# Forty drains of GpSimd between the scatters of a two-mixture kernel

## The chip, the cores and the metric

The kernel runs on one core of a Trainium2 chip. The metric is the device time of one execution in microseconds (us). A run is stated as the median of several executions. The engines are called as the profile calls them: PE is the matrix engine TensorE, DVE is VectorE, ACT is ScalarE, POOL is GpSimd, SP is SyncE. A "q" behind the name (POOLq, SPq) is the engine's sequencer, which fetches instructions, evaluates branches, waits for semaphores and handles some instructions by itself.

## What is computed

The reference has three stages. The first is attention over 8 batches and 8 heads, with keys and values averaged over groups of 8 positions. Its result, 4608 tokens of width 512, goes through a mixture of 8 experts, and the result of that through a second mixture of 8 experts. In each mixture a token goes to the one expert with the largest gate value:

```python
e_idx = np.argmax(logits, axis=1)
for e in range(E):
    mask = e_idx == e
    h = np.maximum(x[mask] @ w1[e], 0.0)
    out[mask] = gate_w[mask, None] * (h @ w2[e])
```

The first mixture has a second, sigmoid gate beside `gate_w`, the second adds a bias by modality to its gate values. Which tokens an expert gets is known on the chip alone, so the kernel sorts the tokens by expert: rows are written by indirect DMAs to places that the chip has computed.

## The kernel before, in words

The attention loop goes over 36 tiles of 128 tokens. When a group of tiles has been routed, `scatter1` (L496) issues one indirect DMA per tile on POOL, which writes the rows into `xs1`, a DRAM buffer with a region for each expert: 36 in all.

Each mixture goes over blocks of 256 sorted rows. `one(s)` (L1000) writes out the work of block `s`; blocks below 18 always run, the others stand in nested conditionals (`rest`, L1092), as many as the counts ask for. PE multiplies in two layers, each with operands split in a high and a low part, three products in place of one. ACT and DVE evict and split. A block's second half of 128 rows stands in a conditional too (`half2`).

POOL has four kinds of work in the mixtures. `bias_of` (L1030) is seven small operations on a block of the first mixture; the last of them, the copy on L865, writes into the row buffer `y`, of which there are two, and so waits for the scatter that read it before. `low2` (L1063, the operations are on L839) makes the low parts of an expert's second-layer weights, 16 operations, in a block that is an expert's last. `scatter()` (defined on L904, the DMA on L907, called on L1065) sends the rows of the block before into `xs2`, the input of the second mixture: one indirect DMA for the first half and one, under a condition, for the second. `write_out` (the DMA on L1080) sends a half block of the second mixture to the output: the first half on L1046, the second under a condition. Where a conditional skips an indirect DMA, the other branch has an INC_SWDGE_SEM on POOLq, which counts the skipped DMA's semaphore up.

The order of the instructions on each engine is the order of the program text. Within `one(s)` that is, for POOL in the first mixture: `bias_of` of block s, then `low2` if the block is an expert's last, then `scatter()` with the rows of block s-1. In the second mixture: `write_out` of the first half, `write_out` of the second, then `low2`.

The program ends with instructions on L1196, after the last line of the kernel's work: on every engine a drain, on SP waits for all semaphores, and barriers between them.

Of the kernel before, what the change touches and what calls it, by code (L numbers as in the profile page):

```python
# [47 lines left out]
def kernel(ctx, tc, q, k, v, wg, wo, w1, w2, mod, wg2, bias2, v1, v2, out):  # L48
    nc = tc.nc
    PE, ACT, DVE, GP, SP = nc.tensor, nc.scalar, nc.vector, nc.gpsimd, nc.sync  # L50
# [64 lines left out]
    def reg(ap, engines, hi):  # L115
        return nc.values_load(ap, engines=engines, min_val=0, max_val=hi, skip_runtime_bounds_check_because=SURE)  # L116
# [90 lines left out]
    def behind(group, ins):  # L207

        for name in placed[group]:
            tc.add_manual_dep(ins.ins, name, DATA, reason="rows that scatters wrote")  # L210
# [555 lines left out]
    def first_layer(xh, xl, between=None):  # L766


        kept = []

        def results(kk, p):
            ACT.activation(HH[kk], p, AF.Relu)  # L772
            DVE.scalar_tensor_tensor(HL[kk], in0=p, scalar=0.0, in1=HH[kk].bitcast(F32), op0=ALU.max, op1=ALU.subtract)  # L773

        after, early, here, then = between or (NF, None, None, None)
        trio = [(W1H, d, xh) for d in range(ND)] + [(W1L, d, xh) for d in (0, 2, 3)] + [(W1H, d, xl) for d in range(ND)] + [(W1L, 1, xh)]
        for kk in range(NF // 2):
            p = pm.tile([P, 2 * BLK], F32, name=f"h{kk}").rearrange("p (c s) -> p c s", c=2)
            for c2 in range(2):
                f = 2 * kk + c2  # L780
                c = f * P
                for n, (W, d, x) in enumerate(trio):
                    PE.matmul(p[:, c2, :], lhsT=W[d][:, c:c + P], rhs=x[:, d, :], start=n == 0, stop=n == 3 * ND - 1)  # L783
                if f == 0 and early:
                    early()
                if f == after:
                    here()
                    for k2, p2 in kept:
                        results(k2, p2)
            if early and 2 * kk + 1 < after:  # L790
                kept.append((kk, p))
                continue
            results(kk, p)
            if kk == after // 2:
                then()
# [21 lines left out]
    def second_layer(hf, p, apart=False):  # L817

        trio = ((HH, W2H), (HH, W2L), (HL, W2H))
        if apart:  # L820
            steps = [(f, trio[i]) for i, fs in ((0, range(NF)), (1, range(NF // 2)), (2, range(NF)), (1, range(NF // 2, NF))) for f in fs]
        else:
            steps = [(f, m) for f in range(NF) for m in trio]
        for i, (f, (X, W)) in enumerate(steps):
            PE.matmul(p, lhsT=X[f // 2][:, f % 2, hf * P:(hf + 1) * P], rhs=W[f // 2][:, f % 2, :], start=i == 0, stop=i == 3 * NF - 1)  # L825

    def weigh(p, hf, S):
        ACT.activation(S["y"][:, hf, 0:DM], p, AF.Copy, scale=S["xg"][:, hf, DM:DM + 1])  # L828

    def split1():  # L830
        for cs in (slice(0, F // 2), slice(F // 2, F)):
            for j in (0, 2, 3, 1):
                split_chunk(R1[j][:, cs], W1H[j][:, cs], W1L[j][:, cs], DVE)
# [15 lines left out]
    def dots(p, S, hf):  # L849


        for e in range(1, E):
            DVE.tensor_tensor_reduce(out=M["junk"][:, e % 2], in0=p, in1=M["wg2b"][:, e, :], scale=1.0, scalar=0.0, op0=ALU.mult, op1=ALU.add, accum_out=S["lg"][:, hf, e:e + 1])  # L853
# [62 lines left out]
    def mixture(m, rows, a1, a2, base, first, after):  # L916
# [20 lines left out]
        def fetch(s):  # L937
            if s >= SMAX:
                return
            if m == 1 and s > 1:  # L940
                DVE.memset(xg_of(s)[:, 1, DM + 1:DM + 2], float(N))
            with run(s, [ET.SP]):
                load_block(s, reg(tabs[0][s:s + 1, ROW:ROW + 1], [ET.SP], E * REG - BLK), half2(s, [ET.SP]))

        def turn_in(s):

            t = turned(pm, ("t0", "t1"))
            xh, xl = x_of(s)
            if s < SMAX:
                with run(s, [ET.PE]) as here:  # L950
                    turn(t, xg_of(s))
            if m == 1 and s >= SMIN:
                with here.Else() if s < SMAX else ExitStack():
                    turn(t, M["xg20"])

            def rest():
                with run(s, [ET.Activation, ET.DVE]) if m == 2 and s < SMAX else ExitStack():
                    if m == 1 or s < SMAX:
                        high(t, xh)
                        low(t, xh, xl)  # L960

            return rest
# [37 lines left out]
        def one(s):  # L1000

            S, T = RS[s % 2], RS[(s - 1) % 2]
            S["xg"] = xg = xg_of(s)
            if SMIN <= s + 1 < SMAX:
                goes_on[s + 1] = reg(tabs[1][s + 1:s + 2, RUN:RUN + 1], ALL, 1)
            if s > 0:
                fetch(s + 3)
                if s > 1:
                    left = turn_in(s + 1)
                p = pm.tile([P, DM], F32, name="y", bufs=2)  # L1010
                with half2(s, C3) as full:
                    first_layer(*x_of(s))
                    second_layer(0, p)
                with full.Else():
                    first_layer_half(*x_of(s))
                    second_layer(0, p, True)
                if s == 1:
                    left = turn_in(2)
                if m == 1:
                    choose(T)  # L1020
                left()
            with when(s, SPLIT1, W3):
                split1()
            if s == 0:
                p = pm.tile([P, DM], F32, name="y", bufs=2)
                second_layer(0, p)
                if m == 1:
                    turn_in(1)()
            if m == 1:
                bias_of(S)  # L1030
            else:
                DVE.tensor_copy(S["ti"], xg[:, :, DM + 1])  # L1032
            weigh(p, 0, S)
            if m == 1:
                if s > 0:
                    scatter = place(T, half2(s - 1, [ET.Pool]))
                if s == SMIN - 2:
                    (fav["order"], fav["ei"], fav["eh"]), fs = favourite(base2, 2)
                    for f in fs:
                        f()  # L1040
                if s == 0:
                    w = M["wg2b"]
                    DVE.tensor_tensor(w[:, 1:E], w[:, 1:E], w[:, 0:1].to_broadcast([P, E - 1, DM]), op=ALU.subtract)
                dots(p, S, 0)
            if m == 2:
                write_out(S, 0)  # L1046
            p1 = pm.tile([P, DM], F32, name="y", bufs=2)
            with half2(s, [ET.PE, ET.Activation, ET.Pool]) if s > 0 else ExitStack():  # L1048
                second_layer(1, p1)
                weigh(p1, 1, S)  # L1050
                if m == 2:
                    write_out(S, 1)
            if s == 0:
                if m == 2:
                    turn_in(1)()
                ahead()
            if m == 1:
                with half2(s, [ET.DVE]) if s > 0 else ExitStack():
                    dots(p1, S, 1)
            with when(s, SPLIT2, [ET.Activation, ET.Pool]):  # L1060
                for j in range(NF // 2):
                    ACT.activation(W2H[j], R2[j], AF.Copy)  # L1062
                low2(range(NF // 2))  # L1063
            if m == 1 and s > 0:
                scatter()  # L1065
            if m == 1 and s == SMIN - 2:
                fav["e"] = reg(fav["ei"][0:1, 0:1], [ET.SP], E - 1)
                row = reg(fav["ei"][0:1, 1:2], [ET.SP], (E - 1) * REG)
                behind("xs2", SP.dma_start(M["xg20"], xs2[ds(row, BLK), :].rearrange("(h p) c -> p h c", p=P)))
                with when(s, LASTE, [ET.SP]):  # L1070
                    load_raw(v1, v2, fav["e"])
            if s + 1 < SMAX:
                with when(s + 1, PF, [ET.SP]):
                    load_raw(a1, a2, reg(tabs[1][s + 1:s + 2, NX:NX + 1], [ET.SP], E - 1))
                if m == 1 and s + 1 >= SMIN - 1:
                    with when(s + 1, PLAST, [ET.SP]):
                        load_raw(v1, v2, fav["e"])

        def write_out(S, hf):
            apart("out", GP.indirect_dma_start(out, IDX(ap=S["ti"][:, hf:hf + 1], axis=0), S["y"][:, hf, 0:DM], None, bounds_check=N - 1, oob_is_err=False))  # L1080
# [120 lines left out]
```

## Time and profile before

| what | us |
|---|---|
| median of 3 runs (1117.98 to 1119.69) | 1118.88 |
| profiled execution, its own time | 1117.44 |
| span of the profile, first to last instruction | 1115.7 |
| PE busy | 1066.5 |
| DVE busy | 594.6 |
| ACT busy | 393.8 |
| POOL busy | 334.7 |

The profile counts an engine as busy while it computes. Register, branch, semaphore and drain instructions are not counted as busy; they appear in the views by line, under the engine's name with a q. A view by line gives for each kind of instruction the count, the shortest, median and longest duration in ns, and the start of the first and of the last. The view in order of time gives start and duration in us and, in brackets, how long the engine had been idle and what released it. The granted clock of TensorE is 0.991 of full speed over the span.

### The profile page before, as it was taken

How to read it: one execution, taken by the hardware profiler on the slowest of the kernel's cores; microseconds unless marked ns; L12 is line 12 of the kernel's file. 1: busy time of each engine (PE TensorE's matmuls, PEld its weight loads, DVE VectorE, ACT ScalarE, POOL GpSimd, SP SyncE). 2: the span in 40 equal slices, each digit the busy share in tenths (PEclk: the TensorE clock that was granted, in tenths of full speed). 3: DMA queues.
4: the chain of work that ended last, by engine and by line, in shares of the span. 5: the costliest groups of instructions: out<-in, count | busy, mean ns of one | idle time of the engine just before them, and what ended most of it. 6: DMA issues, size and time to landing. Idle time of an engine off the chain costs nothing. (4 is left out here: it accounts for less than half of the span.)

```text
span 1115.7 us, 21941 instructions
## 1 busy us (share of the span) xinstructions
PE 1066.5 (96%) x7058; PEld 961.6 (86%) x7058; DVE 594.6 (53%) x1839; ACT 393.8 (35%) x924; POOL 334.7 (30%) x563
## 2 busy tenths in 40 slices
PE   7998989999999999999999989999999999999993
PEld 6998888998888888888888878889998898889982
DVE  6889777768887667679866673211112222111120
ACT  6887872216354215236221151211212512111120
POOL 7566484113757215108312130011000140101000
PEclk9999999999999999999999989999999999999997
DMA  9877455613746114125511005511011211111000
GB/s 345 276 283 250 174 201 189 218 49 123 258 155 225 58 49 161 64 78 163 185 54 41 21 24 177 205 58 58 31 40 39 60 40 39 43 55 40 21 20 22
DMA packets 52096, 128.17 MB, mean 115 GB/s; under 512 B 6957, under 2 KB 10029, under 8 KB 51760
## 3 DMA queue, kind: packets, MB, share of 16 engines
q1 hardware_dynamic: 42928, 97.28, 26.7%
q0 software_dynamic: 8960, 28.47, 6.5%
q8 instruction: 88, 1.44, 0.5%
q14 instruction: 120, 0.98, 0.3%
HBM read 92.51 MB, written 34.27 MB: 114 GB/s over the span
## 5 line engine op out<-in xcount | busy, mean ns | idle before, releaser
L773 DVE SCALAR_TENSOR_TENSOR hl<-h,hh 128x512 fp32r<-128x512 f32 x140 | 95.3, 690 | 368.4 <-ACT hh L772 365.3
L825 PE MATMUL y<-W2H,hh 128*128 128x512 f32 x608 | 235.3, 398 | 2.8 <-ACT W2H L974 2.5
L825 PE MATMUL y<-W2L,hh 128*128 128x512 f32 x608 | 234.6, 395 | 0.5 <-POOL W2L L839 0.5
L825 PE MATMUL y<-W2H,hl 128*128 128x512 f32 x608 | 233.3, 395 | 0.0
L772 ACT ACTIVATE hh<-h 128x512 fp32r<-128x512 f32 x140 | 83.3, 596 | 312.4 <-PE h L783 309.2
L853 DVE CUSTOM_DVE_ANT_0 junk<-y,wg2b 128x512 f32<-128x512 f32 x273 | 169.5, 685 | 8.3 <-ACTq L1060 5.2
L828 ACT ACTIVATE y<-y,xg 128x512 f32<-128x512 f32 x76 | 52.3, 688 | 300.4 <-PE y L825 236.4
L1080 POOL DMA_INDIRECT out_dram<-y,ti x37 | 36.0, 973 | 380.1 <-ACT y L828 258.9
L825 PEld LDWEIGHTS y<-W2H,hh 128*128 128x128 f32 x608 | 114.0, 188 | 28.5 <-ACT W2H L974 2.5
L825 PEld LDWEIGHTS y<-W2H,hl 128*128 128x128 f32 x608 | 114.4, 188 | 26.8
L825 PEld LDWEIGHTS y<-W2L,hh 128*128 128x128 f32 x608 | 114.6, 188 | 26.0 <-POOL W2L L839 1.3
L839 POOL TENSOR_TENSOR W2L<-R,W2H 128x256 fp32r<-128x256 f32 x140 | 99.5, 747 | 84.5 <-ACT W2H L1062 82.2
L783 PE MATMUL h<-xH,W1L 128*128 128x256 f32 x608 | 123.7, 285 | 0.2 <-DVE W1L L193 0.2
L783 PE MATMUL h<-xH,W1H 128*128 128x256 f32 x608 | 100.4, 288 | 4.6 <-issue 3.8
L783 PE MATMUL h<-x2H,W1L 128*128 128x256 f32 x512 | 103.2, 282 | 0.1
L907 POOL DMA_INDIRECT xs<-y,qdi x39 | 39.8, 1020 | 203.3 <-DVE lg L853 190.0
L783 PE MATMUL h<-xL,W1H 128*128 128x256 f32 x608 | 98.5, 285 | 0.0
L783 PEld LDWEIGHTS h<-xH,W1L 128*128 128x128 f32 x608 | 95.8, 193 | 0.4 <-DVE W1L L193 0.4
L783 PEld LDWEIGHTS h<-xH,W1H 128*128 128x128 f32 x608 | 84.7, 194 | 5.0 <-issue 3.8
L783 PEld LDWEIGHTS h<-xL,W1H 128*128 128x128 f32 x608 | 84.6, 194 | 0.0
L783 PE MATMUL h<-x2H,W1H 128*128 128x256 f32 x512 | 83.8, 285 | 0.4 <-ACT x2H L245 0.4
L783 PE MATMUL h<-x2L,W1H 128*128 128x256 f32 x512 | 82.1, 282 | 0.0
(241 smaller groups left out, 1597.1 us busy)
## 6 DMA issues: line engine op xcount, KB each, us to landing
R<-in_w_dram SPq DMA_DIRECT2D x56, 512.0 KB, 4.7
xg<-xs SPq DMA_DIRECT2D x72, 258.0 KB, 2.7
kv<-in_v_dram SPq DMA_DIRECT2D x16, 576.0 KB, 4.5
R<-in_v_dram SPq DMA_DIRECT2D x16, 512.0 KB, 6.3
kv<-in_k_dram SPq DMA_DIRECT2D x14, 576.0 KB, 8.8
qt<-in_q_dram SPq DMA_DIRECT2D x14, 576.0 KB, 10.1
xs<-dummy SPq DMA_DIRECT2D x18, 258.0 KB, 3.5
wraw<-in_w_dram SPq DMA_DIRECT2D x8, 512.0 KB, 4.3
```

The lines of the kernel that those rows point to most:

```text
L772: ACT.activation(HH[kk], p, AF.Relu)
L773: DVE.scalar_tensor_tensor(HL[kk], in0=p, scalar=0.0, in1=HH[kk].bitcast(F32), op0=ALU.max, op1=ALU.subtract)
L783: PE.matmul(p[:, c2, :], lhsT=W[d][:, c:c + P], rhs=x[:, d, :], start=n == 0, stop=n == 3 * ND - 1)
L825: PE.matmul(p, lhsT=X[f // 2][:, f % 2, hf * P:(hf + 1) * P], rhs=W[f // 2][:, f % 2, :], start=i == 0, stop=i == 3 * NF - 1)
L828: ACT.activation(S["y"][:, hf, 0:DM], p, AF.Copy, scale=S["xg"][:, hf, DM:DM + 1])
L839: GP.tensor_tensor(W2L[j][:, c, w], R2[j][:, c, w], W2H[j][:, c, w].bitcast(F32), op=ALU.subtract)
L853: DVE.tensor_tensor_reduce(out=M["junk"][:, e % 2], in0=p, in1=M["wg2b"][:, e, :], scale=1.0, scalar=0.0, op0=ALU.mult, op1=ALU.add, accum ...
L907: apart("xs2", GP.indirect_dma_start(xs2, IDX(ap=di[:, hf:hf + 1], axis=0), y[:, hf, :], None, bounds_check=E * REG - 1, oob_is_err=False))
L1080: apart("out", GP.indirect_dma_start(out, IDX(ap=S["ti"][:, hf:hf + 1], axis=0), S["y"][:, hf, 0:DM], None, bounds_check=N - 1, oob_is_err ...
```

## The change

`GP.drain()` is an instruction on POOL's queue. The change adds two calls in `one(s)`: one in the second mixture ahead of the first half's `write_out`, one in the first mixture ahead of `scatter()`, in all blocks but the first. Nothing else is changed. The `scatter()` that `place` makes in `end` gets none.

```diff
             if m == 2:
+                GP.drain()
                 write_out(S, 0)
...
             if m == 1 and s > 0:
+                GP.drain()
                 scatter()
```

## Rows read from the trace of the kernel before

**Rows 1.** Stages: length; busy us of PE, PEld, DVE, ACT, POOL; clock; DMA share; GB/s.
```profile
669.00:1098.20 429.20, 425.85 (x2708) 383.72 (x2708) 85.39 (x176) 94.47 (x161) 47.24 (x53) 1.00 0.19 61
1098.20:1115.70 17.50, 0.00 (x0) 0.00 (x0) 0.00 (x0) 0.11 (x1) 0.97 (x1) 0.63 0.05 17
```

**Rows 2.** Order of time, the last work: start, us, what, idle before.
```profile
1097.19 0.40 PE L825 MATMUL y<-W2H,hl 128*128 128x512 f32 x1
...
1098.59 0.97 POOL L1080 DMA_INDIRECT out_dram<-y,ti  x1 [4.60 <-ACTq L1060]
```

**Rows 3.** By line, POOL's sequencer from 1100 us on: ns min/median/max, first and last start.
```profile
L1094 POOLq INC_SWDGE_SEM  x1: 2408/2408/2408, 1103.1 to 1103.1; - x1
...
L1196 POOLq DRAIN  x3: 46/107/9223, 1105.7 to 1115.5; - x3
```

**Rows 4.** By line, SP's sequencer from 1105 to 1110 us.
```profile
L1196 SPq EVENT_SEMAPHORE  x12: 28/28/28, 1105.5 to 1106.2; - x12
```

**Rows 5.** By line, all indirect DMAs, who waited for L907's (us, times), the output's landing.
```profile
L497 POOL DMA_INDIRECT xs<-x,rdi x36: 967/993/1240, 48.6 to 178.6; - x36
...
L907 POOL DMA_INDIRECT xs<-y,qdi x39: 967/1061/1066, 216.3 to 669.0; - x39
...
  ACT y L828: 23.7, 4
...
L1080 POOL DMA_INDIRECT out_dram<-y,ti x37: 971/972/993, 680.2 to 1098.6; - x37
...
DMA to landing us min/median/max: 2.7/3.6/3.6
```

**Rows 6.** By line, three other INC_SWDGE_SEM, and the scatters issued before them.
```profile
L1187 POOLq INC_SWDGE_SEM  x1: 31/31/31, 0.2 to 0.2; - x1
...
L907 POOL DMA_INDIRECT xs<-y,qdi x8: 967/1021/1066, 216.3 to 300.2; - x8
...
L906 POOLq INC_SWDGE_SEM  x1: 1074/1074/1074, 307.5 to 307.5; - x1
...
L1080 POOL DMA_INDIRECT out_dram<-y,ti x19: 971/972/980, 680.2 to 887.7; - x19
...
L1048 POOLq INC_SWDGE_SEM  x1: 2039/2039/2039, 888.0 to 888.0; - x1
```

**Rows 7.** By line, POOL's drain ahead of the kernel's work.
```profile
L1187 POOLq DRAIN  x1: 169/169/169, 0.4 to 0.4; - x1
```

**Rows 8.** By line, the instructions whose counts give the number of blocks.
```profile
L859 POOL TENSOR_SCALAR qnm<-xg x22: 186/211/757, 185.7 to 635.1; 128x2 f32<-128x2 f32 x22
...
L1032 DVE CAST ti<-xg x19: 165/169/1379, 679.2 to 1088.9; 128x2 int32<-128x2 f32 x19
```

**Rows 9.** Order of time, POOL in the second mixture, two scatters of results.
```profile
904.48 0.99 POOL L1080 DMA_INDIRECT out_dram<-y,ti  x1 [2.31 <-ACT y L828]
...
1093.01 0.97 POOL L1080 DMA_INDIRECT out_dram<-y,ti  x1 [17.19 <-ACT y L828]
```

**Rows 10.** By line, POOL's sequencer at L907 up to 307.4 us, and 524 to 527.
```profile
L907 POOLq EVENT_SEMAPHORE  x9: 17/17/23906, 191.6 to 306.8; - x9
...
L907 POOLq MOVE  x2: 29/29/29, 525.3 to 526.0; - x2
```

**Rows 11.** Order of time, POOL around two experts' ends in the first mixture.
```profile
287.42 11.27 POOL L839 TENSOR_TENSOR W2L<-R,W2H 128x256 fp32r<-128x256 f32 x16 [1.11 <-ACT W2H L1062]
...
513.88 1.06 POOL L907 DMA_INDIRECT xs<-y,qdi  x1 [0.16 <-ACT W1H L192]
...
520.69 0.56 POOL L865 COPY y<-xg 128x8 f32<-128x8 f32 x1 [0.64 <-DMA xs<-y,qdi]
522.22 11.26 POOL L839 TENSOR_TENSOR W2L<-R,W2H 128x256 fp32r<-128x256 f32 x16 [0.97 <-SPq L1073]
```

**Rows 12.** Order of time, PE's use of the last part of those weights.
```profile
299.90 0.40 PE L825 MATMUL y<-W2L,hh 128*128 128x512 f32 x1
...
534.20 0.40 PE L825 MATMUL y<-W2L,hh 128*128 128x512 f32 x1
```

## The prediction, made before the changed kernel ran

> **What bounds the kernel now.** I read the stages first, then the last work in order of time, then the instructions by line in the stretch in which no engine works, and at last POOL's own order in the mixtures.
>
> In the second mixture PE computes for 425.85 of 429.20 us [rows 1]. What POOL does there costs nothing as long as PE does not wait for it. But the last 17.5 us of the span hold no matmul at all [rows 1]: PE's last one starts at 1097.19, the last scatter of results at 1098.59 [rows 2], it lands at most 3.6 us later [rows 5], so by 1102.2, and the span ends at 1115.7. Some 13 us at the end are neither computation nor transfer.
>
> The views by line show whose they are. POOL's sequencer has an INC_SWDGE_SEM at 1103.1 that lasts 2.41 us, and from 1105.7 on three drains, of which the first lasts 9.22 us, to 1114.9; the other two, 0.11 and 0.05 us, lie in what is left up to 1115.7 [rows 3]. SP, which waits for the kernel's semaphores one after the other, has got through all twelve by 1106.2, 28 ns each [rows 4]: every transfer has landed by then. So for 8.7 us the drain is the one thing that the program's end waits for, and it waits for no data.
>
> What do these two instructions cost by? The kernel issues 36 + 39 + 37 = 112 indirect DMAs on POOL [rows 5]. INC_SWDGE_SEM lasts 1.07 us with 36 + 8 = 44 of them issued before it, 2.04 us with 36 + 39 + 19 = 94 [rows 6], and 2.41 us with all 112 [rows 3]. From the first to the last that is 1.334 us over 68 DMAs, 19.6 ns each; the line gives 2.05 us at 94, where the row has 2.04. It goes by the number of DMAs issued. The drain before the kernel's work, with none issued, lasts 0.17 us [rows 7]; the one behind 112 lasts 9.22 us. If its price too goes by the count, it is 9.05 / 112 = 81 ns for each.
>
> **The change part by part.** The first mixture runs `bias_of` for 22 blocks and the second casts its indices for 19 [rows 8]. The first block of the first mixture has no scatter, so 21 + 19 = 40 drains are added. A block issues one or two indirect DMAs. I take a drain to strike the entries of finished DMAs from a list that grows with each DMA, so that later instructions find the list short. The row at the end is the only long drain here, so that is a reading and not yet shown.
>
> *The end.* The last added drain stands ahead of the last block's first scatter. Behind it come two DMAs. The final drain then lasts 0.17 + 2 x 0.081 = 0.33 us in place of 9.22. SP is late next: its waits end 0.7 to 0.8 us behind the INC_SWDGE_SEM (1105.5 to 1106.2 [rows 3, 4]), and the drain only 0.5 us behind it. From the drain's end to the end of the span it is 1115.7 - 1114.9 = 0.8 us, and stays.
>
> *The INC_SWDGE_SEM ahead of it.* If it goes over the same list, it falls to the line's value at two DMAs, 1.074 - 42 x 0.0196 = 0.25 us; the shortest row is 0.03 us [rows 6]. I take 0.2, so it ends at 1103.3 and no longer at 1105.5. If it counts all DMAs of the execution, it stays at 2.41.
>
> *Sum.* 1103.3 + 0.8 (SP) + 0.8 (end) = 1104.9 of span in place of 1115.7: 10.8 us less. With the INC_SWDGE_SEM unchanged it is 1105.5 + 0.8 + 0.8 = 1107.1, 8.6 less.
>
> *The drains in the second mixture.* Each costs POOL 0.17 + 2 x 0.081 = 0.3 us by the count, and holds its sequencer until the engine is idle and, at worst, until the DMAs before it have landed (3.6 us [rows 5]). The scatter behind it has POOL idle 17.19 us ahead of it in the last block, and 2.31 us where `low2` stands before it [rows 9], waiting for ACT's result. Both cover 0.3 us, and behind `low2` the earlier DMAs have long landed. Cost nothing; without the cover, nobody in the second mixture waits for a scatter of results but the end.
>
> *The drains in the first mixture.* The first one strikes the 36 entries of `scatter1`: 0.17 + 36 x 0.081 = 3.1 us. POOL's sequencer waits up to 23.9 us at the scatters for DVE [rows 10], which hides that and the later drains of 0.3 us. It is different where `low2` runs directly before the drain. There the sequencer now runs ahead: it prepared the two scatters at 525.3 and 526.0, while `low2` was still running until 533.48 [rows 10, 11]. With the drain it must wait for the last `low2` operation and 0.33 us more, and then prepare the scatter; today that gap is 0.16 us [rows 11]. I bound the shift from 0.3 us (the preparation hidden in today's gap) to 1.0 us (preparation of both scatters exposed, 0.7 us apart in rows 10), and take 0.4, by the drain's row. Behind the scatter on POOL are `bias_of`, whose copy at 520.69 waits for the landing, and where two experts end in a row the next `low2`, 522.22 [rows 11]. PE waits for that: its use of what the last two operations write starts at 534.20, and `low2` ends at 522.22 + 11.26 = 533.48: a slack of 0.72 us. At the other such place it is 299.90 - (287.42 + 11.27) = 1.21 us [rows 11, 12]. A shift of 0.4 is hidden at both; at 1.0 the first costs 0.3 us. ACT waits four times for a scatter's landing, 23.7 us in all [rows 5], and would wait 0.4 longer; PE has a second `y` buffer to go on with, so I count nothing. The INC_SWDGE_SEM within the mixtures (1.07 and 2.04 us in rows 6) get shorter too, which can give back no more than PE idles: 429.20 - 425.85 = 3.35 us in the whole second mixture [rows 1]. At those two PE goes on as before, so I count none. Together: 0, from -1.2, a third of that idle time, to +1.
>
> The Trainium skill states on the page "PSUM — Partial Sum Buffer", section "Engine vs sequencer instructions", that a drain waits for the engine to go fully idle. The trace does not bear that out as the whole of it: POOL's last work ended at 1099.56, 6.1 us before the 9.22 us drain began [rows 2, 3]. By that rule alone the final drain would be no shorter and the sum would be nothing.
>
> **The sum against the runs.** The profiled execution took 1117.44 us, 1.7 more than its span, and would take 1106.6. The median of the runs is 1118.88; less 10.8 that is 1108.1. I forecast 1108.1 us.
>
> **The rivals.**
>
> *The INC_SWDGE_SEM stays.* For it: it is a count of DMAs issued in every row, and no drain stands between any two of them to show what a drain does to it. Against: it is simplest if both walk one list. Time 1118.88 - 8.6 = 1110.3.
>
> *The end is fixed.* The 9.22 us could be a cost of ending the program that has nothing to do with the count; there is one such row, and INC_SWDGE_SEM's slope is another instruction's. Against: the two drains behind it are also of POOL and of the end, and take 0.11 and 0.05 us [rows 3]. Time 1118.9, no change. The Trainium skill, page "Runtime: NRT & Kernel Launch", section "The ~15µs preamble/postamble breakdown", describes barriers and resets around any kernel by stage, about 9 to 15 us in total; by that table the end would stay. It names no stage that grows with the kernel's DMAs.
>
> *Each drain walks all DMAs issued so far* (slower). Then nothing is struck off, the final drain stays 9.22 us, and the drains in the body grow. At 513.88 some 36 + 25 DMAs have been issued (25 of the 39 by their even spread over 216.3 to 669.0 [rows 5]): 0.17 + 61 x 0.081 = 5.1 us, against 0.72 us of slack: PE loses 4.4. Ahead of 287.42 it is 36 + 5, 3.5 us, less 1.21 is 2.3. Time 1118.9 + 6.7 = 1125.6. It decides from the point where the drain ahead of 513.88 is longer than about 0.7 us. For it: a walk over everything issued is what INC_SWDGE_SEM's rows look like. Against: a drain that left nothing cleared would have to be 9 us again right behind the first one at the end, where they take 0.11 and 0.05.
>
> *The body costs more than it seems.* A drain that takes 2 us and not 0.3 for a few DMAs would push both `low2` places: 1.3 + 0.8 = 2.1 us. Time 1110.2.
>
> **How the numbers follow.** Chances: the forecast 0.67, the INC_SWDGE_SEM stays 0.13, the body costs more 0.05, the end fixed 0.08, each drain walks all 0.07. A difference of about 0.2%, 2.2 us, is what a measurement of this kernel can tell from none. The first three are faster by more than that: 0.85. Same 0.08, slower 0.07. The range takes in the first three: below, the forecast less the 1.2 and the runs' own scatter (0.9 either way), 1106.0; above, 1110.3 with the body's +1 and the scatter, 1112.3. That leaves out 0.15 and a little at the edges.
>
> **What would show it.** In the changed kernel's rows by line: the last POOL drain well under 1 us and the last INC_SWDGE_SEM near 0.2; SP's last waits, and no longer POOL's drain, directly ahead of the end; some 6 us from the last scatter of results to the end of the span and not 17; the forty drains about 0.3 us each and the first of them about 3; the scatter behind `low2` some 0.5 us behind its end; PE's gaps in the mixtures as before. The prediction is wrong if the final drain is still several us long, if the drains in the body grow along the kernel, or if PE waits for `low2` behind 522.22.

## The result and the profile after

The changed kernel takes 1109.48 us (median of 4 runs, 1108.82 to 1110.16), the kernel before, run beside it, 1119.29 us. The ratio is 0.9908 with a 95% interval of 0.9888 to 0.9928: faster by some 10 us. The forecast was 1108.1 us, with a range of 1106.0 to 1112.3.

| what | before, us | after, us |
|---|---|---|
| profiled execution, its own time | 1117.44 | 1110.16 |
| span of its profile | 1115.7 | 1108.4 |
| last matmul ends | 1097.6 | 1101.3 |
| from there to the end of the span | 18.1 | 7.1 |
| PE busy | 1066.5 | 1068.8 |

The table already shows two things: the end has become 11.0 us shorter, and TensorE finishes 3.8 us later. The first is what was forecast. The second was not.

The stage at the end, the whole second mixture beside it; columns as in [rows 1]:

```profile
669.00:1101.40 432.40, 427.57 (x2712) 385.11 (x2710) 86.50 (x192) 95.27 (x162) 47.37 (x54) 1.00 0.18 61
1101.40:1108.40 7.00, 0.00 (x0) 0.00 (x0) 0.00 (x0) 0.67 (x1) 0.97 (x1) 0.64 0.12 42
```

By line, the count instruction (INC_SWDGE_SEM) behind the last blocks, POOL's drains at the end and SP's waits, from three answers on three lines (columns: ns min/median/max, first and last start); they answer to [rows 3, 4]:

```profile
L1096 POOLq INC_SWDGE_SEM  x2: 213/214/215, 671.9 to 1106.3; - x2
...
L1198 SPq EVENT_SEMAPHORE  x14: 17/28/393, 1106.4 to 1108.4; - x14
...
L1198 POOLq DRAIN  x3: 46/107/208, 1106.7 to 1108.2; - x3
L1198 SPq DRAIN  x3: 7/7/13, 1107.6 to 1107.9; - x3
```

The longest of the three drains of POOL at the end takes 0.21 us where it took 9.22, and the INC_SWDGE_SEM 0.215 where it took 2.41. POOL's drain is over at 1106.9. SP's waits go on to 1107.5 (one of them lasts 0.39 us) and its drain comes at 1107.6, so SP is now late, as the prediction said it would be.

The added drains, by line, the first mixture's and then the second's. An indirect DMA is called open here as long as no drain has come behind it, whether it has landed or not:

```profile
L1066 POOLq DRAIN  x21: 122/218/8468, 190.5 to 642.2; - x21
...
L1046 POOLq DRAIN  x19: 302/2164/7853, 678.2 to 1080.4; - x19
```

Of the 21 in the first mixture 13 take 0.12 to 0.22 us. The shortest, with one indirect DMA since the drain before, lasts 0.12 us, those with two 0.21, and the first, with 36, 3.02 us: about 0.05 us and 0.083 us for each DMA. Seven of them last 8.4 to 8.5 us. These stand behind `low2`: the sequencer reaches the drain while `low2` is running and stays there until its last operation is over. POOL in order of time around two such places, then the scatter's line and the drain's line:

```profile
509.45 4.95 POOL L839 TENSOR_TENSOR W2L<-R,W2H 128x256 fp32r<-128x256 f32 x7
515.52 1.06 POOL L907 DMA_INDIRECT xs<-y,qdi  x1 [1.12 <-DVE qkm L879]
...
523.09 0.19 POOL L865 COPY y<-xg 128x8 f32<-128x8 f32 x1 [1.75 <-DMA xs<-y,qdi]
524.62 11.25 POOL L839 TENSOR_TENSOR W2L<-R,W2H 128x256 fp32r<-128x256 f32 x16 [1.34 <-ACT W2H L1063]
537.00 1.06 POOL L907 DMA_INDIRECT xs<-y,qdi  x1 [1.12 <-DVE qkm L879]
```

```profile
L907 POOLq MOVE  x2: 29/29/29, 514.7 to 515.4; - x2
...
L1066 POOLq DRAIN  x1: 8435/8435/8435, 506.2 to 506.2; - x1
```

`low2` ends at 509.45 + 4.95 = 514.40, the drain at 506.2 + 8.44 = 514.6, and only then does the sequencer begin on the scatter (the first MOVE, 514.7). The scatter starts at 515.52, so POOL has idled 1.12 us where it idled 0.16 before [rows 11]. The releaser that the view names, DVE's `qkm`, is not the cause, although it is ready only at 515.39, shortly ahead of the scatter. In the kernel before the scatter does not wait for it: it starts at 513.88 [rows 11], and that `qkm` comes behind it:

```profile
514.54 0.17 DVE L879 TENSOR_REDUCE qkm<-qa 128x2 f32<-128x16 f32 x1
```

So the time is the sequencer's own. The next `low2` then starts at 524.62, 2.40 us later than before [rows 11]. Of that, 0.68 us was there ahead of the drain (the `low2` in front of it ends at 514.40 and ended at 513.72). TensorE now reaches the products of `low2` first:

```profile
534.53 0.50 PE L825 MATMUL y<-W2L,hh 128*128 128x512 f32 x1 [0.18 <-POOL W2L L839]
...
535.93 0.50 PE L825 MATMUL y<-W2L,hh 128*128 128x512 f32 x1 [0.43 <-POOL W2L L839]
...
537.34 0.18 PE L886 MATMUL h<-oh,tri_b 128*128 128x16 bf16 x1 [0.68 <-DVE oh L881]
...
537.88 0.50 PE L825 MATMUL y<-W2H,hh 128*128 128x512 f32 x1 [0.31 <-issue]
```

This is the order of time of PE with the idle time before each in brackets: 1.60 us in four waits. The last of them, 0.31 us, the kernel before has too (0.30). The third, for DVE's `oh`, belongs to `low2` as well. DVE in order of time in the same stretch:

```profile
531.27 4.77 DVE L874 SCALAR_TENSOR_TENSOR qlg<-lg,y,bs 128x8 f32<-128x8 f32 x2
...
537.11 0.17 DVE L881 TENSOR_TENSOR oh<-qa,va 128x16 bf16<-128x16 f32 x1
```

Two small operations take 4.77 us there and end at 536.04; the first of them takes 4.63 and ends at 535.90, with `low2` (524.62 + 11.25 = 535.87); the median one takes 0.22 us. The kernel before shows the same, and how little room it left:

```profile
530.59 2.92 DVE L874 SCALAR_TENSOR_TENSOR qlg<-lg,y,bs 128x8 f32<-128x8 f32 x1
...
534.72 0.18 DVE L881 TENSOR_TENSOR oh<-qa,va 128x16 bf16<-128x16 f32 x1
```

```profile
534.95 0.18 PE L886 MATMUL h<-oh,tri_b 128*128 128x16 bf16 x1
```

There the operation on L874 ends at 533.51, with `low2` (533.48 [rows 11]), `oh` is written by 534.90, and TensorE takes it at 534.95. So `low2`'s end reaches TensorE by two ways, by its own products and by `oh`, and the second had 0.05 us of slack. Not every operation of DVE is held up like this: the 26 on L773 that ran beside `low2` took 0.67 to 0.69 us, as the others do.

In the second mixture the first drain lasts 0.30 us, with three open DMAs, the one behind `low2` 7.9, with one, and the others 1.4 to 4.3 us, with two each. Take one of these. The second half's scatter starts at 1055.06 and lands 2.7 us after its issue, by 1057.8; the drain that follows runs from 1056.5 to 1057.9. It waits for the landing: here and in twelve others of the nineteen the drain ends 0.12 us behind it.

```profile
1055.06 0.97 POOL L1082 DMA_INDIRECT out_dram<-y,ti  x1 [4.60 <-ACTq L1061]
1073.03 0.97 POOL L1082 DMA_INDIRECT out_dram<-y,ti  x1 [17.00 <-ACT y L828]
```

The next scatter starts at 1073.03 and has 17.00 us of POOL's idle time ahead of it, for ACT. That is the cover the prediction named; it hides 2 us as it would 0.3.

### The profile page after: what moved, and what is told of

It is laid out like the page before. It is cut to its first block, busy times and chain, and to the rows that moved or that the text cites. A ratio compares the mean times of both kernels' runs of the same rounds, so it can differ in the third digit from the quotient of the medians.

```text
span 1108.4 us, 21981 instructions
## 1 busy us (share of the span) xinstructions
PE 1068.8 (96%) x7058; PEld 963.7 (87%) x7058; DVE 594.1 (54%) x1839; ACT 393.6 (36%) x924; POOL 333.4 (30%) x563
## 5 line engine op out<-in xcount | busy, mean ns | idle before, releaser
L773 DVE SCALAR_TENSOR_TENSOR hl<-h,hh 128x512 fp32r<-128x512 f32 x140 | 95.3, 690 | 366.3 <-ACT hh L772 365.0
L907 POOL DMA_INDIRECT xs<-y,qdi x39 | 39.8, 1021 | 209.7 <-DVE lg L853 194.4
```

The source lines that it names most:

```text
L907: apart("xs2", GP.indirect_dma_start(xs2, IDX(ap=di[:, hf:hf + 1], axis=0), y[:, hf, :], None, bounds_check=E * REG - 1, oob_is_err=False))
```

## The experiments

Two questions were open: what in the body takes back part of the gain, and by what the end's price goes. All ratios are to the kernel before on the same chip.

**The change again, beside its parts.** Theory A: where the drain stands behind `low2`, it holds the sequencer, the scatter and the next `low2` come late, and TensorE loses about 2 us. Theory B: the loss was a lower clock of that one execution.

> The changed kernel again, as the measure for the others of this call. 9.8 us under the kernel before (ratio 0.991). Theory A: two places where low2 follows the scatter of the block before cost it about 2 us of PE's time, because POOL's sequencer prepares the scatter only behind the drain; PE's waits for W2L and for oh show again. Theory B: that loss was this one execution's lower clock, and another execution does not show it.

Measured: 1109.78 us (6 runs), ratio 0.9927 (0.9912 to 0.9943); before 1117.98. TensorE's waits near 302 and from 536 to 539 us are there again.

**The drains of the second mixture alone.**

```diff
             if m == 1 and s > 0:
-                GP.drain()
                 scatter()
```

> Drains in the second mixture alone. Both theories: the first of them strikes 75 entries (0.05 + 75 x 0.083 = 6.3 us), the last drain and INC_SWDGE_SEM are as short as with the change (0.2 us each). Theory A: no wait of PE behind low2 is added in the first mixture, so it is 11 us under the kernel before and 1 to 2 us under the changed one. Theory B: the same time as the changed one, 9.8 under.

Measured: 1109.2 us, ratio 0.991 (0.9895 to 0.9924). The waits in the first mixture are gone. The time is not told apart from the whole change's.

**The drain of the first mixture ahead of `low2`.** The same number of drains, none behind `low2`.

```diff
+            if m == 1 and s > 0:
+                GP.drain()
             with when(s, SPLIT2, [ET.Activation, ET.Pool]):
...
             if m == 1 and s > 0:
-                GP.drain()
                 scatter()
```

> Both groups of drains, those of the first mixture ahead of the condition with low2 and not behind it. Theory A (the sequencer held behind low2 costs): the scatters start 0.2 us behind low2 again, PE's added waits go, 10.5 to 11 us under the kernel before. Theory B: the same as the changed one.

Measured: 1107.03 us, ratio 0.9906 (0.9891 to 0.9921). POOL in order of time at the place shown above:

```profile
508.45 5.66 POOL L839 TENSOR_TENSOR W2L<-R,W2H 128x256 fp32r<-128x256 f32 x8
514.27 1.06 POOL L907 DMA_INDIRECT xs<-y,qdi  x1 [0.16 <-ACT W1H L192]
...
522.90 11.27 POOL L839 TENSOR_TENSOR W2L<-R,W2H 128x256 fp32r<-128x256 f32 x16 [1.26 <-ACT W2H L1065]
```

The scatter is back at 0.16 us behind `low2`, the kernel before's gap. The busy time of PE by stretch, first the kernel with the whole change run again, then this one, then the one with a single drain (below), settles Theory A at this place:

```profile
290.00:310.00 20.00, 19.02 (x112) 16.19 (x111) 14.28 (x41) 6.68 (x12) 14.13 (x25) 1.00 0.71 235
525.00:545.00 20.00, 18.61 (x107) 15.30 (x106) 15.40 (x48) 5.88 (x11) 14.71 (x25) 1.00 0.16 50
```

```profile
290.00:310.00 20.00, 20.00 (x117) 17.21 (x116) 13.10 (x41) 4.20 (x8) 13.00 (x23) 1.00 0.66 209
525.00:545.00 20.00, 20.00 (x125) 17.62 (x124) 15.77 (x55) 4.24 (x9) 15.02 (x31) 1.00 0.18 55
```

```profile
525.00:545.00 20.00, 20.00 (x125) 17.55 (x124) 15.53 (x55) 4.25 (x8) 13.53 (x28) 1.00 0.20 64
```

From 525 to 545 us TensorE idles 1.39 us with the drain behind `low2` (1.60 in the first profile of the change) and not at all with it ahead; the granted clock is 1.00 in every row, so Theory B does not account for these waits. The seven other traces agree: 0.86 us with the first mixture's drains alone, at most 0.42 in those without a drain behind `low2`, the kernel before included. From 290 to 310 us the picture is less clean: 0.57 to 0.98 us with it, but 0 to 1.17 without, because in two of these (38 more and 2 more, below) about 1 us of waiting that the other traces have near 281 us is absent and a wait comes behind 298 us instead. The first mixture as a whole, 220 to 640 us, parts the two groups. First the whole change run again, then the kernel with the drain ahead of `low2`:

```profile
220.00:640.00 420.00, 412.91 (x2641) 365.90 (x2640) 312.22 (x1004) 144.85 (x264) 149.13 (x284) 1.00 0.34 113
```

```profile
220.00:640.00 420.00, 415.72 (x2645) 370.00 (x2644) 309.84 (x1007) 145.22 (x263) 149.51 (x280) 0.99 0.34 113
```

TensorE idles 6.6 to 7.1 us there in the three traces with a drain behind `low2` (the change twice, and the first mixture's drains alone), and 4.1 to 5.2 in the eight without, of which the kernel before has the 5.2: 6.8 against 4.4 in the mean, 2.4 us apart. Both places have a part in it: from 220 to 310 us it is 2.4 to 3.1 with it and 1.5 to 2.2 without.

In time, the six runs of the whole change have a mean of 1110.4 us and the five of this kernel 1107.7; the difference of 2.7 us has an interval of 0.7 to 4.7, worked out from their scatter. This is the weaker evidence: in its first measurement the changed kernel had a ratio of 0.9908, no worse than the 0.9906 of this one.

**One drain only**, in the second mixture two blocks ahead of the end.

```diff
             if m == 2:
-                GP.drain()
+                if s == SMIN - 1:
+                    GP.drain()
                 write_out(S, 0)
...
             if m == 1 and s > 0:
-                GP.drain()
                 scatter()
```

> One drain in the whole program, in the second mixture's block 17, ahead of its first scatter. If a drain strikes the finished entries off a list, it lasts about 9 us in POOL's idle time, four scatters follow, the last drain is 0.05 + 4 x 0.083 = 0.4 us and the whole is 10.8 to 11 us under the kernel before. If the end were fixed, or every scatter needed its drain, it would be no faster than the kernel before.

Measured: 1107.21 us, ratio 0.990 (0.9886 to 0.9914). By line, the drain, the count instructions and the end:

```profile
L1047 POOLq DRAIN  x1: 8897/8897/8897, 1052.8 to 1052.8; - x1
...
L1096 POOLq INC_SWDGE_SEM  x2: 248/950/1653, 669.9 to 1103.1; - x2
...
L1198 POOLq DRAIN  x3: 46/107/381, 1103.5 to 1104.7; - x3
```

The 8.90 us have moved to 1052.8, into POOL's wait of 17 us, and behind them four DMAs are left: 0.38 us. One drain gives the whole gain of the end. By the scatter of its runs it is 3.3 us under the whole change in the mean (interval 1.5 to 5.1); against the one with the drains ahead of `low2` nothing can be told.

**The drains of the first mixture alone.**

```diff
             if m == 2:
-                GP.drain()
                 write_out(S, 0)
```

> The drains of the first mixture alone, those of the second left out. If a drain costs 0.05 us and 0.083 us for each indirect DMA of GpSimd since the last drain, and the count instruction 0.21 us and 0.0196 us for each (fitted to the trace of the changed kernel), the last drain here has the 37 indirect DMAs since the last drain before it: 0.05 + 37 x 0.083 = 3.1 us, and the count instruction 0.21 + 37 x 0.0196 = 0.93 us. The tail behind TensorE's last matmul is then 18.1 - (9.2 - 3.1) - (2.4 - 0.9) = 10.5 us. Theory A (the drains behind the low2 products hold the sequencer and cost TensorE some 1.4 us at 535-538 us and 0.6 us at 301 us): TensorE's waits of 0.4 and 0.7 us behind low2 are there as in the changed kernel, the span is about 1115.7 - 7.6 + 2 = 1110 us, and the time about 5.6 us under the kernel before. Theory B (those waits were that execution's alone): they are absent and the time is 7.6 us under it. Rival for the end (it costs the same however many DMAs are open): last drain 9.2 us, no gain.

Measured: 1112.18 us, ratio 0.995 (0.9938 to 0.9963), 5.7 us under the kernel before, where 5.6 was expected.

```profile
L1095 POOLq INC_SWDGE_SEM  x2: 213/592/972, 670.2 to 1104.6; - x2
...
L1197 POOLq DRAIN  x3: 52/111/3412, 1106.2 to 1110.2; - x3
```

The expectation left out three DMAs: behind the last added drain come the two of its own `scatter()`, one that `place` makes in `end`, and the 37 of the second mixture, so 40 are open. The last drain takes 3.41 us (0.05 + 40 x 0.083 = 3.4) and the count instruction 0.97 (0.21 + 40 x 0.0196 = 0.99). The end's price goes by the number since the last drain, and the rival of a fixed end falls. That the time came out as expected is in part luck, since the end was forecast 0.3 us too short.

**38 more indirect DMAs and no drain.** This should have been the mirror image: two more ahead of each block's first `write_out`, with indices out of bounds, so that they write nothing.

```diff
+    away = cst.tile([P, 1], I32, name="away")
+    GP.iota(away, [[1, 1]], base=OOB, channel_multiplier=1)
...
             if m == 2:
+                for _ in range(2):
+                    apart("out", GP.indirect_dma_start(out, IDX(ap=away, axis=0), dummy[:, 0:DM], None, bounds_check=N - 1, oob_is_err=False))
                 write_out(S, 0)
```

> The kernel before, without any drain, with two more indirect DMAs of GpSimd ahead of each block's first scatter of results in the second mixture, whose indices are all out of bounds so that they write nothing: 38 more, 150 in all. If the end grows by each indirect DMA issued since the last drain, the last drain takes 0.05 + 150 x 0.083 = 12.4 us (9.2 before) and the last count instruction 0.21 + 150 x 0.0196 = 3.15 us (2.4 before), the tail behind TensorE's last matmul is 3.9 us longer, and the time some 3.9 us above the kernel before (ratio 1.0035), as far as the 38 themselves are hidden behind TensorE. Rival (the end has a fixed price, or goes by bytes written): last drain 9.2 us, and a time equal to the kernel before.

Measured: 1110.6 us, ratio 0.9933 (0.9916 to 0.9949). Neither what was expected nor its rival: it is faster than the kernel before by 7 us, without a drain.

```profile
L1052 POOLq INC_SWDGE_SEM  x1: 319/319/319, 892.5 to 892.5; - x1
...
L1098 POOLq INC_SWDGE_SEM  x2: 1074/1364/1653, 671.1 to 1105.5; - x2
...
L1200 POOLq DRAIN  x3: 46/107/3670, 1106.8 to 1111.0; - x3
```

The count instruction takes 1.65 us at 671.1, behind 75 DMAs, but 0.32 at 892.5 behind 114, and the last drain's 3.67 us stand for (3.67 - 0.05) / 0.083 = 44 DMAs, not 150. Some 106 were dropped on the way. Theory C says that GpSimd drops entries by itself when about 113 are kept; Theory D, that DMAs which write nothing do it. Three kernels tell the reasons apart: 2 more and 8 more of the same kind (one in each of the first blocks of the second mixture), and 38 that do write.

```diff
+                if s < 2:
+                    apart("out", GP.indirect_dma_start(out, IDX(ap=away, axis=0), dummy[:, 0:DM], None, bounds_check=N - 1, oob_is_err=False))
                 write_out(S, 0)
```

> As the kernel with 8 more, but only 2 more, in the first two blocks of the second mixture: 114 in all. Theory C, with the limit at 113 or 114: the entries are dropped at the last DMAs of the kernel, the last drain is at most 1 us instead of 9.2 and the last count instruction at most 0.4 us, some 10 us less in all. If the limit lies above 114 the last drain takes 0.05 + 114 x 0.083 = 9.5 us and the time is that of the kernel before. Theory D: the entries fall at the second block, the last drain then has 36 of them and takes 3 us, the time some 7.5 us less.

Measured with 2 more: 1110.75 us, ratio 0.9927 (0.9899 to 0.9954); before 1118.52.

```profile
L1052 POOLq INC_SWDGE_SEM  x1: 2087/2087/2087, 890.0 to 890.0; - x1
...
L1098 POOLq INC_SWDGE_SEM  x2: 328/990/1653, 671.1 to 1107.2; - x2
...
L1200 POOLq DRAIN  x3: 46/107/730, 1107.7 to 1109.0; - x3
```

For 8 more the condition is `s < 8`.

> The kernel before, no drain, with one more indirect DMA of GpSimd (all indices out of bounds, nothing written) in each of the first 8 blocks of the second mixture: 120 in all. Theory C (GpSimd keeps one entry for each indirect DMA, and when some 113 of them are kept it drops the finished ones without a drain; the kernel before stops at 112, just under it): the count instruction at about 888 us, behind 102 DMAs, still takes 0.21 + 102 x 0.0196 = 2.2 us, then the entries fall to about ten, the last drain takes 0.05 + 14 x 0.083 = 1.2 us and the last count instruction 0.5 us, and the time is some 10 us under the kernel before. Theory D (each DMA that writes nothing clears the entries, or leaves a cheaper one): the count instruction at 888 us is already at 0.5 us or so, the last drain about 2 us. Theory E (the gain of the 38 came from something else than this list): last drain 9.9 us, and no gain.

Measured: 1108.34 us, ratio 0.9916 (0.9899 to 0.9933).

```profile
L1052 POOLq INC_SWDGE_SEM  x1: 2199/2199/2199, 889.3 to 889.3; - x1
...
L1098 POOLq INC_SWDGE_SEM  x2: 452/1052/1653, 670.8 to 1104.4; - x2
...
L1200 POOLq DRAIN  x3: 46/107/1220, 1105.0 to 1106.8; - x3
```

The kernel with 38 that write differs in the target and the indices, and it gives the DMAs a group of their own:

```diff
+    spare = dram.tile([64 * P, DM], F32, name="spare")
+    spared = []
...
+    away = cst.tile([P, 64], I32, name="away")
+    GP.iota(away, [[P, 64]], base=0, channel_multiplier=1)
...
             if m == 2:
+                for _ in range(2):
+                    k = len(spared)
+                    spared.append(k)
+                    apart("spare", GP.indirect_dma_start(spare, IDX(ap=away[:, k:k + 1], axis=0), dummy[:, 0:DM], None, bounds_check=64 * P - 1, oob_is_err=False))
                 write_out(S, 0)
```

> As the kernel with 38 more, but the 38 write: each puts 128 rows of zeros into a DRAM tensor of its own, every index in bounds; 150 in all. Theory C (the number of DMAs alone): as with the 38 that write nothing, count instructions of 0.32 us at 892 us and 1.07 us at the end, last drain 3.7 us, time some 7 us under the kernel before, less what the 38 x 256 KB cost where TensorE waits for a transfer (nothing in the second half, by the DMA share of the page). Theory D (the ones that write nothing did it): last drain 0.05 + 150 x 0.083 = 12.5 us, count instruction 3.15 us, time 4 us above the kernel before.

Measured: 1111.34 us, ratio 0.9936 (0.992 to 0.9953).

```profile
L1204 POOLq DRAIN  x3: 46/107/3670, 1106.8 to 1111.1; - x3
```

The 38 that write give the same last drain as the 38 that don't, 3.67 us: what they write does not matter, and Theory D falls. The count instruction behind 96 and 102 DMAs is still at 2.09 and 2.20 us. With 114, 120 and 150 DMAs the last drain takes 0.73, 1.22 and 3.67 us, which at 0.05 + 0.083 each is 8, 14 and 44 entries: each time 106 are missing. So GpSimd drops 106 entries by itself at the 114th DMA or the one before it, without a drain. It does not drop every finished one: with 2 more, the 113th starts at 1095.44 and the one before it at 1077.22, so all but one of the 113 ahead had landed long since, and yet seven stay. Nor is the drop free. POOL in order of time with 2 more, a usual second half and then the 114th DMA, the last of the program:

```profile
1077.22 0.97 POOL L1084 DMA_INDIRECT out_dram<-y,ti  x1 [4.62 <-ACTq L1064]
...
1102.51 0.98 POOL L1084 DMA_INDIRECT out_dram<-y,ti  x1 [6.10 <-issue]
```

The 114th has 6.10 us of idle time ahead of it where others have 4.6; with 8 more it is again the 114th, and again 6.10. With 2 more it starts 2.46 us behind the end of the last matmul where the kernel before has 1.00: about 1.5 us for the drop, which lie in the end there and in the middle of the mixture with 8 more. Theory C stands. The kernel before, with 112, ends just short of that point and has the longest last drain of all.

## Why the prediction was right

*The end.* Right in both terms and in its reason. The drain went to 0.21 us (0.33 forecast) and the INC_SWDGE_SEM to 0.215 (0.2). SP came last, as forecast. The tail is 11.0 us shorter where 10.8 were forecast. The reading behind it, a list that a drain clears and that both instructions walk, was only read from rows; the experiments with 40, 4 and 2 open entries bear it out, and the first drain with the second mixture's drains alone, 6.20 us for 75. The two rivals in which the end or the count instruction stays are refuted by [rows 3] beside their answers above, and the one in which each drain walks all DMAs by drains of 0.2 us late in the first mixture, behind 70 DMAs.

*The drains in the second mixture.* Right in the cost, zero, and in the cover: from 690 to 1097 us TensorE is busy for 405.81 us where it was 405.87. The size was too low: 0.3 us was forecast, and 17 of the 19 last 1.4 to 4.3 us, the wait for the landing that the prediction had as its worst case.

*The first drain.* 3.02 us where 3.1 were forecast, hidden: it ends at 193.6, and the scatter behind it starts at 215.5.

*The drains behind `low2`: the term that was mis-sized.* The prediction had the right place and the right mechanism, but took a shift of 0.4 us out of 0.3 to 1.0, and let the slack of 0.72 us hide it. POOL's idle time ahead of the scatter rose by 1.12 - 0.16 = 0.96 us, near the upper bound: 0.24 us from `low2`'s end to the drain's, and 0.88 us that the sequencer needs before its scatter runs. A drain takes away the running ahead, and I priced the drain but only half of what is lost with it. On its way the shift grew in two of the three traces: from the scatter's start to the start of `low2` it is 9.10 us, and 8.91 with the change run again, where it was 8.34 [rows 11], because the copy on L865 now waits 1.75 and 1.55 us for the landing. With the first mixture's drains alone it is 7.81, although the gap of 1.12 us is the same there, so the growth is not shown to come from the drains, and the waits are there without it (0.86 us).

The larger error is the slack. The prediction took 0.72 us from TensorE's use of `low2`'s products. It did not see that DVE's `oh` depends on `low2` too, and there the slack was 0.05 us. (The trace of before shows that way in another place: behind the `low2` that ends at 279.4 TensorE waits 0.91 us for `oh`.) So a shift that 0.72 us would have hidden reached TensorE, which waits 0.9 to 1.6 us from 525 to 545 us instead of the 0.4 of the kernel before. That TensorE waits for `low2` behind 522.22 was one of the prediction's own signs of being wrong; for this term it was wrong. Undoing that one thing, the drain ahead of `low2`, takes the waits away. The body's sum was forecast as 0, from -1.2 to +1 (the 1.2 was called a third of 3.35, which is 1.1). By TensorE's idle time in the first mixture it is about +2.4 against the traces without a drain behind `low2`, and +1.4 to +1.9 against that of the kernel before. The forecast of the time held because this is small beside the end.

The rival in which the body costs more had about that size, 2.1 us, and those places, but not the cause: it wanted drains of 2 us for a few DMAs, and these take 0.2.

*What stays open.* In the profile of after TensorE ends 3.8 us later than in that of before; 1.5 us of that are the idle time from 220 to 640 us. The end of its last matmul lies between 1097.6 and 1100.6 us in the seven experiments' traces without a drain behind `low2`, and the edits don't explain its order, so the rest of the 3.8 us is taken to be the scatter of single executions; that was not tested. Why DVE's small operation on L874 ends with `low2` is not shown either.

The Trainium skill's statement, on the page "PSUM — Partial Sum Buffer", section "Engine vs sequencer instructions", that a drain waits for the engine to go fully idle, is borne out by the seven drains of 8.4 us that end with `low2`. It is not the whole: the one at 1056.5 waited for a DMA's landing while POOL was idle, and the one of 8.90 us in the single-drain kernel lasted far longer than a landing of results takes (2.7 to 3.6 us in [rows 5]).

## What to carry to other kernels

Look at what stands behind the last matmul: a drain of several us, there or anywhere, may be the price of bookkeeping that piled up earlier, and one drain placed in a long wait of the same engine moves all of it there. A drain's price is not its own duration alone but also the running ahead of the sequencer that it ends; put it ahead of long work on its engine, not between that work and something that others wait for. And look for every reader of the work that is shifted before you call a shift hidden: here one way had 0.72 us of slack and the other 0.05.

## What the runs showed of the hardware

- A drain of GpSimd took 0.05 us and 0.083 us for each indirect DMA issued since the last drain (3.02 us for 36, 3.41 for 40, 6.20 for 75, 8.90 for 108, 9.22 for 112), INC_SWDGE_SEM about 0.2 us and 0.02 us for each (0.97 for 40, 2.41 for 112). The drain also waited for the last one's landing and ended 0.12 us behind it.
- Without any drain the entries fell by 106 at the 114th DMA or the one before it; the 114th started about 1.5 us late, and seven entries stayed of which at most one was of a DMA still under way. Two more indirect DMAs that write nothing therefore made the kernel before about 8 us faster (ratio 0.9927, 0.9899 to 0.9954), about as much as the forty drains.
- The sequencer took 0.88 us from the end of a drain to the start of the scatter behind it. Where it could run ahead of `low2` the scatter started 0.16 us behind it.
- A small operation of DVE (L874, 0.22 us in the median) that met the long runs of `low2` on GpSimd took up to 4.6 us and ended with them, in the kernel before as in the changed one. The larger ones on L773 ran beside `low2` at their usual 0.69 us.
